# Polysketch attention with a multiplicative FFN: w3 loaded in row blocks, warm-up, key features and instruction order changed

## The chip, the cores and the metric

The kernel runs on one core of one Trainium2 chip. The metric is device time in microseconds (us), the median of three runs. A profiled execution gives the span from the first to the last instruction and the rows that are read below.

## The reference

Inputs q, k, v are (4, 4, 1088, 32), S1 and S2 are (8, 32), w1 and w2 are (128, 1024), w3 is (1024, 1024), w_out is (1024, 128). q, k, v are float32; S1, S2 and the weights come as float64, which the kernel reads as pairs of 32-bit words.

```python
def phi(x):                       # 64 features from 32 numbers
    a = np.einsum('rd,bhsd->bhsr', S1, x)
    b = np.einsum('rd,bhsd->bhsr', S2, x)
    return np.einsum('bhsi,bhsj->bhsij', a, b).reshape(*x.shape[:-1], r * r)
q_p, k_p = phi(q), phi(k)
kv = np.einsum('bhsf,bhsd->bhfd', k_p, v)
z = np.sum(k_p, axis=2)
num = np.einsum('bhsf,bhfd->bhsd', q_p, kv)
den = np.einsum('bhsf,bhf->bhs', q_p, z)[..., None] + 1e-06
attn_out = num / den
x = attn_out.transpose(0, 2, 1, 3).reshape(4352, 128)
out = ((x @ w1) * (x @ w2)) @ w3 @ w_out
```

## The kernel before

The whole program is a set of named steps, each of which issues one or a few instructions on one engine (or one or a few transfers). `ORDER`, a long string of step names, says in which order they are issued; every engine works its own instructions strictly in that order, and so does each engine's transfer queue. A step that must wait holds all later steps of its engine.

**Weights.** There are eleven weight tiles of 128 x 1024 words of 64 bits: w0 and w1 hold halves of w1 and w2 together, w2 is w_out, w3 to w10 are the eight row blocks of w3. Step `wN.load` (in `conv`) brings a tile into `raw`, of which there are three buffers. ACT turns it into float32 in three steps, `wN.c` (L325, upper word scaled), `wN.s` (L329, sign bits) and `wN.m` (L333, lower word); DVE finishes with `wN.j` (L344) and `wN.a` (L349). The `raw` buffer is free after `wN.c` and `wN.m`. The tiles of w3 are loaded in four transfers that each fill 32 partitions.

**Folding.** w3 and w_out are multiplied first: for each block ko, `fK.t` (DVE, L377) transposes the w3 tile in 32 x 32 blocks, `fK.m` (PE, L383) makes eight products with `wo`, and `fK.o` (ACT) puts the result into `w3o`.

**FFN.** The 4352 rows are worked in eight groups g0 to g7 of 512 columns and a rest gr of 256. For each group and each of eight column blocks c: `gG.Ca` and `gG.Cb` (PE, L1099 and L1109) make the products with w1 and w2, `gG.Cc` (ACT, L1104) copies the first, `gG.Cm` (DVE, L1115) multiplies the two into an `ab` tile (17 buffers), and `gG.Co` (PE, L1121) adds its product with `w3o[c]` to the group's output. `gG.oT` transposes the output, and `gG.st` stores it in four transfers; the output tile has one buffer.

**Attention.** For batch b the `kB.` steps make the key side. `kB.max`, `kB.lead` and `kB.rest` split k in a coarse and a fine part, `kB.gram0` to `gram2` sum its outer products (PE, L492), and a chain of small steps (`G..`, `T..`, `N..`) makes scaled projections from them. `kB.kT`, `kB.ab` and `kB.kp` make the features, `kB.kv` multiplies them with v, and `kB.kz` is what a query needs of a batch. `krM.` steps do the last 64 rows of two batches. `qG.` steps make the query side of group G, ending with `qG.x` (PE) and `qG.xT` (ACT), whose output `xT` the FFN products of group G read. For batch 0 the features `k0.kp0` and `k0.kp1` are made by GpSimd (POOL), one instruction each (L515).

**Zero products.** Steps `warm0` to `warm8` give PE products of zeros with zeros (L176), as many as `WARM` says, at places set in `ORDER`. They lie ahead of the first FFN product.

**Transfers** are all issued by SP, but for the two loads of k for batch 0, which ACT issues.

Of the kernel before, what the change touches and what calls it, by code (L numbers as in the profile page):

```python
# [25 lines left out]
WARM = [15, 5, 3, 1, 6, 15, 4, 2, 5]  # L26
# [7 lines left out]
c.zeros v0.zero c.ident c.mask k0.zero k0.load0 k0.loadr k0.load1 s.load c.act q0.load s.zero v0.loadr w0.load  # L34
k0.max0 w1.load k0.max1 k0.nat1 kr0.load warm0 k0.tr1 k0.g0 k0.g1 k0.lead0 k0.kT1 k0.lead1 kh1.load k0.nat0
k0.rest0 s.words k0.rest1 warm1 k0.gram0 s.pair q0.tr s.split k0.gram1 q1.tr s.lead w0.c v0.load q0.max k0.tr0
k0.Gm s.T k0.Gt k0.kT0 w0.j k1.zero s.P k1.load q0.l2 s.blk k0.Ga s.blkh warm2 k0.ab1 k0.Gb q0.l1 s.Pp k1.loadr
q0.A0 k0.ab0 w2.load q0.rm k0.T0 k0.T1 k0.abc0 kr0.tr k0.abc1 k0.Ta k0.kp0 warm3 q0.C0 w1.c k1.kT1 q1.max w1.m
k0.Tb q0.sma q0.restT kr0.kT k0.Ts w0.m k0.kp1 warm4 k0.kv0 k1.max k0.N0 k0.N1 w0.s q0.sta w3.load k0.Na q0.sha
w1.s k0.Nh k0.Nb q0.sla kr1.load warm5 q0.A1 k0.Nl k0.Nf kr0.ab q0.sca k0.kv3 q0.smy kr0.abc q0.al k0.kv1 kr0.kp  # L40
q0.sty q0.C1 q0.phi w4.load q1.l2 k0.kv2 k0.kvr v1.zero q1.l1 q0.shy warm6 q0.pt0 k0.kvm q0.C1t q0.sly k0.kzt
q0.pt1 q0.pc0 q0.scy v1.load q0.p01 q1.A0 k0.kz q0.pc1 q0.p2 warm7 q0.x q1.rm q0.p12 w1.j w3.c q0.dn q0.de w2.c
q1.sm q1.C0 q0.rc q1.st q0.xs w0.a q0.xt q0.xT q1.sh w2.m k1.g w1.a warm8 g0.1a g0.1b w2.j g0.1c w5.load w2.s
k1.lead g0.0a g0.1m kr1.tr g0.6a kr1.kT g0.0c k1.rest w3.s g0.0b w2.a kr1.ab g0.6b g0.6c w3.m g0.5a g0.0m g0.6m
g0.7a g0.5c w6.load q1.sl kr1.abc k1.kT0 g0.5b w3.j g0.7b g0.5m q1.load w4.c k1.gram0 w3.a g0.7c k1.ab w4.m
q1.sca q1.scy f0.t k1.gram1 w5.c w7.load k1.gram2 q1.al q1.p01 g0.2a q1.p2 w4.s k2.zero g0.7m q1.p12 kh2.load
g0.4a w4.j g0.2c q1.dn f0.m g0.4c w4.a w6.c k2.load q1.de k1.Gm f1.t v1.loadr w5.m g0.2b g0.4b q1.rc g0.2m f0.o
w5.s w10.load f1.m k1.Gt q1.bs q2.tr w6.m q1.phi g0.0o k1.abt f1.o w6.s w8.load q1.pt1 k1.Ga q2.max q1.pt0 w5.j
g0.3a q1.pc0 g0.4m q1.pc1 k2.loadr q1.x k1.kp1 g0.1o q1.xT w5.a q2.l2 g1.1a g0.3c k1.Gb g0.3b f2.t g1.1c q2.l1
k1.T0 k1.T1 g1.5a g0.3m f2.m k1.Ta g1.5c k1.kp0 w7.c w7.m w6.j g1.1b k1.Tb g1.6a w6.a f2.o w7.s w9.load k1.kv0  # L50
g1.1m k1.kv2 k1.kv3 k1.kv1 w8.c w7.j k1.kvr g0.2o f3.t w8.s g1.5b w7.a f3.m g1.6c k1.kvm k1.Ts g1.5m w8.j g1.6b
f3.o f4.t k1.N0 w9.c k1.N1 g1.4a g1.6m g1.4b k1.Na g1.4c k2.max w9.s f4.m g1.4m w8.m k1.Nb g1.0a k2.g w9.j f4.o
g1.0b k1.Nf q2.rm g1.0c w10.c k2.lead g0.3o k1.Nl k1.Nh g1.3a g1.0m k2.rest g1.2a g1.3c w9.m g0.4o q3.tr w8.a
k2.gram0 k2.gram1 k2.kT1 q2.C0 f5.t k2.kT0 k2.gram2 q3.max q2.A0 k2.ab k3.zero k3.loadr v2.zero w9.a kr1.kp
q3.l2 v2.load f5.m g1.2c q2.At q3.l1 q2.Ct q2.sm q3.rm g1.7a f5.o w10.s q2.st f6.t g1.3b w10.m g0.5o q2.sh w10.j
f6.m q2.sl g1.3m q2.sca q2.scy q2.al q3.A0 q2.p01 f6.o q3.C0 g1.7c w10.a g1.2b q2.p2 f7.t g1.7b q2.p12 q2.dn
f7.m k2.Gm q2.de q1.restT q2.rc q2.load q2.bs q3.At v2.loadr q3.Ct g0.6o kh3.load q2.phi f7.o g0.7o k2.abt
q2.pt0 k3.load g0.oT q2.pt1 g1.2m k1.kzt g1.0o g0.st k1.kz q2.pc0 q3.sm g1.7m q2.pc1 g1.2o k2.Gt q3.st g1.5o
q3.sh q3.sl q2.x k2.kp0 g1.3o q2.xT q3.sca k3.max g2.7a g2.1a k3.g k2.Ga q3.p01 k2.kp1 g2.7b g2.1c g2.7c g1.1o
q5.tr g1.6o q5.max q3.al k3.lead g1.4o q4.tr g1.7o k2.Gb g2.5a g2.7m q4.max g2.1b q3.scy k3.rest g2.5b k2.kv0  # L60
q3.p2 k3.gram0 g2.1m q3.p12 g2.5c k3.gram1 k3.kT0 g2.5m k2.kv3 k2.kv1 k2.kv2 g1.oT k2.kvr k3.gram2 v3.zero
v3.load k2.kvm q3.dn k2.T0 k2.T1 g2.2a k3.Gm k2.Ta g2.3a k2.Tb v3.loadr g2.2c k2.Ts q3.de q4.l2 g1.st q3.rc
k2.N0 q3.bs k2.N1 q3.phi g2.2b q4.l1 g2.3c g2.0a g2.2m k2.Na g2.3b g2.0c k2.Nb q3.pt1 k2.Nh k3.kT1 g2.0b g2.3m
q3.pt0 q4.rm g2.6a k2.Nf g2.0m g2.4b g2.6c k3.Gt k2.Nl q3.pc0 g2.4a q3.pc1 q3.x q4.A0 q3.xT q4.C0 g2.4c k3.ab
g2.0o k3.abt g2.4m g3.3a g2.6b g2.2o g2.6m k3.Ga g3.3b q4.At g3.3c q4.sm g2.5o q4.st q4.Ct g3.2b g3.3m q4.sh
g3.2a k3.kp0 k2.kzt g2.1o g3.2c q5.l2 g3.2m g3.4a k3.kp1 g2.4o g3.4c k2.kz q4.sl q5.l1 g3.4b q4.sca k3.Gb g3.6a
q4.p01 g3.4m q5.A0 q4.al k3.T0 k3.T1 g3.1a k3.Ta q5.At g2.6o q4.scy g3.1c q5.sm g3.6c q5.rm g3.1b q2.restT
q3.load g2.3o g3.1m k3.Tb g3.0b q4.p2 q4.p12 g3.6b q4.dn q4.de k3.Ts q5.st g3.0a q5.sh q3.restT g2.7o g3.0c
g3.0m q5.C0 q4.rc g3.6m q5.sl k3.kv0 k3.kv1 g2.oT k3.kv3 k3.kv2 q4.bs k3.kvr g2.st q5.Ct g3.5a q5.sca q5.p01
g3.7b g3.5c q6.tr g3.0o q4.phi g3.5b k3.kvm q7.tr g3.3o q5.al qr.max g3.2o q5.scy qr.l2 g3.5m q5.p2 q4.pt0  # L70
q5.p12 g3.6o q5.dn q4.pc0 qr.l1 g3.7a q4.pt1 g3.7c g3.1o q4.pc1 g3.7m q4.x q5.de q5.rc q5.bs g3.4o q4.xT k3.N0
k3.N1 g4.3b k3.Na qr.rm g4.3a k3.Nh k3.Nf k3.Nb q5.phi g4.0a g4.3c g3.5o g4.3m g4.0c q5.pt0 g4.5a g4.5b g4.5c
q5.pc0 q5.pt1 g4.5m g3.7o q5.pc1 g4.0b g4.4a g4.0m g3.oT g4.4b g4.4c g3.st g4.2a g4.4m k3.Nl g4.7a q6.max g4.0o
qr.C0 qr.A0 q5.x qr.Ct qr.At q7.max g4.5o q5.xT qr.sm g4.2c g4.2b g4.7c q6.l2 g4.7b g4.2m q6.l1 qr.st g5.0a
g4.7m qr.sh g4.6a g5.0c qr.sl q6.rm k3.kzt g4.6b qr.sca k3.kz g4.6c qr.al qr.p01 g5.0b g4.6m q6.A0 g5.0m q6.C0
q6.At qr.scy qr.p2 q7.l2 g4.1a qr.p12 qr.dn qr.de qr.rc g4.2o g4.1c q7.l1 g4.6o q7.rm g4.3o q6.sm qr.bs g4.1b
g5.2a g4.1m qr.phi g5.2b g5.2c q6.st qr.pt0 q6.sh g5.7a qr.pc0 q6.sl q6.Ct g4.4o g5.2m qr.pt1 q6.sca g4.1o
qr.pc1 q6.al g5.7c g5.7b q7.A0 q7.C0 q7.At q6.p01 g5.7m qr.x q6.scy q6.p2 q6.p12 g5.5a q6.dn q6.de q6.rc g4.7o
g5.5c q6.bs g5.6a g4.oT g5.6b g4.st g5.6c qr.xT g5.0o g5.6m q7.sm g5.5b q7.st g5.4a g5.5m q7.sh g5.4b g5.4c
q6.phi g5.5o q7.Ct g5.1a g5.4m q6.pt0 g5.3b q6.pc0 q6.pt1 g5.3a q6.pc1 g5.1c q6.x g5.3c g5.3m g5.1b q6.xT g5.6o  # L80
g5.1m q7.sl g5.4o q7.sca g5.1o g5.3o g6.1a g5.2o g6.1c g6.1b g6.4a g6.1m q7.scy g6.6a q7.al g6.4c q7.p01 g6.4b
g6.6c g5.7o g6.4m q7.p2 g6.6b g5.oT q7.p12 g6.0a g5.st g6.6m q7.dn g6.0b g6.0c g6.5a g6.0m g6.3a g6.5c g6.3b
g6.3c g6.5b g6.3m q7.de gr.2b g6.5m g6.0o q7.rc q7.bs g6.2a q7.phi gr.2a g6.2c g6.4o gr.2c gr.2m g6.6o g6.2b
gr.0a g6.2m q7.pt1 gr.0b gr.0c q7.pt0 gr.0m g6.7a q7.pc0 g6.7b g6.7c q7.pc1 q7.x g6.7m g6.5o q7.xT g7.1a g7.1b
g7.1c g7.0a g7.1m g6.2o g7.3a g6.3o g7.3c g7.0c g7.0b g6.1o g7.0m g6.7o g7.3b g6.oT g7.4a g6.st g7.3m g7.4b
g7.4c g7.2b g7.4m g7.2a g7.6a g7.2c g7.2m g7.0o g7.6c g7.2o g7.5a g7.1o g7.5c g7.6b g7.7a g7.6m g7.5b g7.7c
gr.5a g7.5m g7.7b gr.6a g7.7m g7.5o gr.6c gr.5c g7.3o gr.6b gr.5b g7.6o gr.5m gr.6m gr.4b gr.4a g7.4o gr.4c
gr.4m gr.1b gr.1a g7.7o gr.1c gr.1m gr.3a g7.oT gr.3b gr.3c gr.7a g7.st gr.3m gr.0o gr.7c gr.6o gr.2o gr.5o
gr.7b gr.3o gr.7m gr.1o gr.4o gr.7o gr.oc gr.ot gr.oT gr.st
# [7 lines left out]
def make_steps(ctx, tc, q, k, v, S1, S2, moe_w1, moe_w2, moe_w3, moe_w_out, out):  # L97
    nc = tc.nc
    dve, act, pe, pool, sp = nc.vector, nc.scalar, nc.tensor, nc.gpsimd, nc.sync
    B, H, S, D = q.shape  # L100
    r = S1.shape[0]
# [190 lines left out]
    def conv(n):  # L292
# [3 lines left out]
        def _():  # L296
# [4 lines left out]
            elif n == 2:  # L301
                for t in range(4):
                    sp.dma_start(raw[n][t * 32:(t + 1) * 32],
                                 bass.AP(tensor=moe_w_out.tensor, offset=moe_w_out.offset + t * 256 * DM,
                                         ap=[[DM, 32], [32 * DM, NC], [1, DM]]))
            elif n - 3 in BY_PE:
                sp.dma_start(raw[n], moe_w3[(n - 3) * 128:(n - 2) * 128])
            else:
                for t in range(4):
                    sp.dma_start(raw[n][t * 32:(t + 1) * 32],  # L310
                                 bass.AP(tensor=moe_w3.tensor, offset=moe_w3.offset + (n - 3) * 128 * DF + t * 256,
                                         ap=[[DF, 32], [32 * DF, 4], [1, 256]]))
# [898 lines left out]
```

## Time and profile before

| | us |
|---|---|
| median of 3 runs (279.46 to 284.89) | 280.36 |
| the profiled execution | 279.55 |
| its span | 277.70 |
| PE busy | 261.6 (94%) |
| DVE busy | 186.0 (67%) |
| ACT busy | 113.0 (41%) |
| POOL busy | 11.6 (4%) |

Busy time counts an instruction from its start to its end; products on PE overlap, so that a busy PE is not PE at its peak. In the page of the profile the span is cut into 40 equal slices, 6.9 us each; a digit is the busy share of a slice in tenths. DMA is the mean busy share of the 16 DMA engines. 22.5 MB are moved in all, 19.9 MB of them read from memory, nearly all in the first 75 us. Rows of a timeline give start and duration in us, engine, line, operation, output and inputs, shape and count, and in brackets how long the engine was idle before and what ended it; "issue" there is time in which it waited for nothing that the profile shows.

### The profile page before, as it was taken

The numbers are of one execution on the slowest core, as the hardware profiler recorded it, in microseconds if no ns is written. First come the engines' busy times: TensorE is split into PE (matmuls) and PEld (weight loads), VectorE is DVE, ScalarE is ACT, GpSimd is POOL, SyncE is SP. The second block draws the span as 40 slices with busy tenths as digits, with TensorE's granted clock in tenths as the row PEclk, the third lists the DMA queues.
The fourth block names the chain that finished last, engine by engine and source line by source line (L and its number), as shares of the span: only waits on it lengthen the run. The fifth ranks groups of instructions, "written<-read, shape, count | busy, mean of one in ns | idle before, by whom it ended". The sixth has DMA issues, their size and how long they took to land.

```text
span 277.7 us, 5298 instructions
## 1 busy us (share of the span) xinstructions
PE 261.6 (94%) x2134; PEld 147.7 (53%) x2134; DVE 186.0 (67%) x420; ACT 113.0 (41%) x180; POOL 11.6 (4%) x41
## 2 busy tenths in 40 slices
PE   7997899699998999979999999999999999999992
PEld 5886646446657663634444544444544445344571
DVE  4779989699889999965597944576772264132330
ACT  3576599676592522034132134154223222322121
POOL 2451000000001000000000000000000000000000
PEclk9999999999999999999999999999999999999998
DMA  7999989999500273050002200200020020011011
GB/s 202 341 257 210 206 192 251 211 218 200 123 1 19 66 211 65 2 120 0 2 0 81 40 0 0 40 0 1 2 38 0 0 41 0 0 19 19 0 21 38
DMA packets 32168, 22.50 MB, mean 81 GB/s; under 512 B 21392, under 2 KB 26640, under 8 KB 32144
## 3 DMA queue, kind: packets, MB, share of 16 engines
q1 hardware_dynamic: 31600, 21.64, 34.8%
q10 hardware_dynamic: 544, 0.52, 0.6%
q8 instruction: 17, 0.28, 0.5%
q14 instruction: 7, 0.06, 0.1%
HBM read 19.93 MB, written 2.23 MB: 80 GB/s over the span
## 4 chain that ended last, share of the span: by engine, by line
PE 68%; DMA 22%; SPq 3%; ACT 3%; issue 2%; DVE 0%; ACTq 0%
PE ps_o L1121 19%; PE a_ps L1099 18%; PE b_ps L1109 18%; DMA raw<-in_moe_w_dram 15%; DMA k<-in_k_dram 6%; PE ps_c L810 3%; PE ps_w3o L383 3%; PE ps_x L1065 3%; PE ps_ph L1020 2%; PE ps_g L492 1%; SPq L1077 1%; ACT sg L333 1%; ACT cv_c L325 1%; PE ps_kv L590 1%; DMA out_dram<-oT 1%
## 5 line engine op out<-in xcount | busy, mean ns | idle before, releaser
L1115 DVE TENSOR_TENSOR ab<-ffa,b_ps 128x512 f32<-128x512 f32 (+1 forms) x72 | 46.9, 652 | 59.3 <-PE b_ps L1109 45.5
L1104 ACT COPY ffa<-a_ps 128x512 f32<-128x512 f32 (+1 forms) x72 | 39.9, 565 | 97.0 <-PE a_ps L1099 85.4
L1099 PE MATMUL a_ps<-xT,w 128*128 128x512 f32 (+1 forms) x144 | 69.1, 575 | 1.6 <-ACT xT L1057 1.2
L1109 PE MATMUL b_ps<-xT,w 128*128 128x512 f32 (+1 forms) x144 | 68.8, 572 | 0.0
L1121 PE MATMUL ps_o<-ab,w3o 128*128 128x512 f32 (+1 forms) x144 | 67.4, 574 | 0.0
L1109 PEld LDWEIGHTS b_ps<-xT,w 128*128 128x128 f32 x144 | 26.4, 190 | 28.4 <-issue 24.9
L1099 PEld LDWEIGHTS a_ps<-xT,w 128*128 128x128 f32 x144 | 25.8, 190 | 27.5 <-issue 20.2
L1121 PEld LDWEIGHTS ps_o<-ab,w3o 128*128 128x128 f32 x144 | 26.1, 190 | 26.2 <-issue 23.1
L383 PEld LDWEIGHTS ps_w3o<-wo,w3T 128*128 128x128 f32 x128 | 15.5, 192 | 6.6 <-issue 5.4
L383 PE MATMUL ps_w3o<-wo,w3T 128*128 128x128 f32 x128 | 16.1, 277 | 2.4 <-issue 2.4
L325 ACT ACTIVATE cv_c<-raw 128x1024 f32<-128x1024 f32 x11 | 12.8, 1174 | 7.2 <-DMA raw<-in_moe_w_dram 7.2
L333 ACT ACTIVATE sg<-raw 128x1024 uint16<-128x1024 uint32 x11 | 15.2, 1380 | 0.0
L329 ACT CAST sg<-cv_c 128x1024 f16<-128x1024 f32 x11 | 15.0, 1378 | 0.0
L1026 ACT COPY pT<-ps_ph 128x512 f32<-128x512 f32 (+1 forms) x18 | 9.9, 566 | 7.4 <-PE ps_ph L1020 7.2
L492 PE MATMUL ps_g<-kk 128*32 128x64 f32 x288 | 10.8, 232 | 1.8 <-issue 1.8
L1020 PEld LDWEIGHTS ps_ph<-ident,ph 128*128 128x128 f32 x68 | 8.2, 141 | 6.8 <-issue 4.6
L492 PE MATMUL ps_g<-k,kk 128*32 128x32 f32 x288 | 10.3, 200 | 1.1 <-issue 1.1
L176 PE MATMUL idle_ps<-zeros 128*128 128x256 bf16 x56 | 9.8, 326 | 1.1 <-DVE zeros L151 1.1
L492 PEld LDWEIGHTS ps_g<-kk 128*32 128x32 f32 x288 | 9.0, 114 | 3.2 <-issue 1.9
L492 PEld LDWEIGHTS ps_g<-k,kk 128*32 128x32 f32 x288 | 9.6, 116 | 1.9 <-issue 1.9
L1020 PE MATMUL ps_ph<-ident,ph 128*128 128x128 f32 x68 | 10.1, 274 | 0.0
L377 DVE STREAM_TRANSPOSE w3T<-w3c 128x1024 f32<-128x1024 f32 x8 | 9.9, 1235 | 0.0
(199 smaller groups left out, 290.9 us busy)
## 6 DMA issues: line engine op xcount, KB each, us to landing
raw<-in_moe_w_dram SPq DMA_DIRECT2D x32, 256.0 KB, 7.9
qh<-in_q_dram SPq DMA_DIRECT2D x4, 544.0 KB, 4.1
raw<-in_moe_w_dram SPq DMA_DIRECT2D x4, 512.0 KB, 6.1
out_dram<-oT SPq DMA_DIRECT2D x32, 64.0 KB, 2.0
kh<-in_k_dram SPq DMA_DIRECT2D x12, 128.0 KB, 6.8
k<-in_k_dram SPq DMA_DIRECT2D x3, 512.0 KB, 7.3
v<-in_v_dram SPq DMA_DIRECT2D x12, 128.0 KB, 2.8
raw<-in_moe_w_out_dram SPq DMA_DIRECT2D x4, 256.0 KB, 8.0
```

The source lines that it names most:

```text
L325: act.mul(shape(x["c"], 1, True), words(1).bitcast(F32), 2.0 ** -112)
L329: act.copy(bview(sign_bits[n % 2].bitcast(F16)[:, 1:], [[2, 1024]]), x["c"])
L333: act.mul(shape(sign_bits[n % 2].bitcast(U16), 2, True), words(0).bitcast(U32), 2.0 ** -29)
L377: dve.transpose(w3T[ko].rearrange("p s (i r) -> p s i r", r=32), bview(w3c[ko], [[32, NC], [256, 4], [1, 32]]))
L383: pe.matmul(t["o"], w3T[ko][:, c], wo[:, c], start=c == 0, stop=c == NC - 1)
L492: pe.matmul(o[h * D:(h + 1) * D], lhs, rhs, start=start, stop=stop, skip_group_check=True)
L1020: pe.transpose(t[:, j * 128:(j + 1) * 128], ph_cols(j, p), ident)
L1099: pe.matmul(x["a"][:, :w], w_of(0, c), xT[g][:, c0:c0 + w], start=True, stop=True)
L1104: act.copy(x["s"][:, :w], x["a"][:, :w])
L1109: pe.matmul(x["b"][:, :w], w_of(1, c), xT[g][:, c0:c0 + w], start=True, stop=True)
L1115: dve.tensor_mul(ab_sb[g, c][:, c0:c0 + w], x["s"][:, :w], x["b"][:, :w])
L1121: pe.matmul(o_ps[g][:, :n], w3o[:, c], ab_sb.pop((g, c))[:, :n], start=c == 0, stop=c == NC - 1)
```

## The change

Four things change. The w3 tiles are still loaded in four transfers each, of the same size, but one transfer now takes 32 whole rows of w3 and fills 256 columns of all 128 partitions. The zero products are 19, 5, 2, 3, 18, 6 and 5 in seven places, where they were 15, 5, 3, 1, 6, 15, 4, 2 and 5 in nine. The features of batch 0 are made by GpSimd in halves (`k0.kp0a`, `k0.kp0b`, `k0.kp1a`, `k0.kp1b`). And `ORDER` is another one; to allow for it, the transposed keys `kT` are kept by batch. No other step is different.

```diff
-WARM = [15, 5, 3, 1, 6, 15, 4, 2, 5]
+WARM = [19, 5, 2, 3, 18, 6, 5]
...
-                for t in range(4):
-                    sp.dma_start(raw[n][t * 32:(t + 1) * 32],
-                                 bass.AP(tensor=moe_w3.tensor, offset=moe_w3.offset + (n - 3) * 128 * DF + t * 256,
-                                         ap=[[DF, 32], [32 * DF, 4], [1, 256]]))
+                for i in range(4):
+                    sp.dma_start(raw[n][:, i * 256:(i + 1) * 256],
+                                 bass.AP(tensor=moe_w3.tensor, offset=moe_w3.offset + ((n - 3) * 128 + i * 32) * DF,
+                                         ap=[[256, 4], [DF, 32], [1, 256]]))
...
-                @step(f"k{b}.kp{half}")
-                def _(half=half):
-                    f["kp", half] = sb("kp", [128, 4 * H, r, r], bufs=2)
-                    x = f["abs", half]
-                    k_phi(f["kp", half], x[:, 0], x[:, 1], pool)
+                for part in "ab":
+                    @step(f"k{b}.kp{half}{part}")
+                    def _(half=half, part=part):
+                        if part == "a":
+                            f["kp", half] = sb("kp", [128, 4 * H, r, r], bufs=2)
+                        x, g = f["abs", half], slice(0, 2 * H) if part == "a" else slice(2 * H, 4 * H)
+                        k_phi(f["kp", half][:, g], x[:, 0, g], x[:, 1, g], pool)
```

In a pattern such as `[[DF, 32], [32 * DF, 4], [1, 256]]` each pair is a step and a count, the outermost first.

The order of SP's first loads was k0 rest, S, q0, v0 rest, w0, w1, kr0, kh1, v0, k1, k1 rest, w2, w3, kr1, w4, v1, w5, w6, q1, w7, kh2, k2, v1 rest, w10, w8, k2 rest, w9. It is now k0 rest, S, q0, kh1, kr0, w0, k1, k1 rest, v0, w1, w3, v0 rest, w2, k2, w5, kr1, w4, w7, v1, k2 rest, q1, w6, kh2, w8, w9, v1 rest, k3, w10. (khB is k once more in another layout, for `kB.kT`.)

The opening of the new order up to the first FFN products, and its end:

```
c.zeros c.ident s.zero k0.zero k0.load1 k0.loadr k0.load0 c.mask s.load c.act q0.load kh1.load k0.max1 kr0.load
k0.max0 k0.nat0 s.words warm0 k0.tr0 k0.g0 k0.lead0 w0.load k0.g1 k0.rest0 k0.lead1 warm1 k0.gram0 s.pair
...
k0.kT1 k0.kp0a k0.Gb k1.max k0.kp0b kr0.tr k0.T0 k0.T1 kr0.kT w0.c k0.Ta v0.zero v0.load w1.load w3.load
v0.loadr q0.sma w0.m k1.g w0.j k0.Tb q0.sta w0.s warm4 k0.N0 k0.Ts w2.load k1.lead k0.ab1 q0.sha k1.rest w1.c
k0.N1 k0.kv0 kr0.ab k0.kv1 k0.Na kr0.abc w1.m k1.gram0 kr0.kp q0.sla k0.Nb k1.gram1 q0.sca w1.s k0.Nf k0.Nh w0.a
q0.A1 k0.abc1 k0.Nl q0.C1 q0.al w3.c q0.smy k0.kp1a k1.kT1 q0.sty q1.l2 q0.phi k0.kp1b warm5 k0.kv2 k1.gram2
q1.l1 q0.shy k0.kv3 q0.C1t k2.zero k2.load k0.kvr q0.sly q0.pt0 k0.kvm w5.load v1.zero q0.scy q1.A0 q0.p01
k0.kzt q0.pc0 q0.pt1 w1.j k1.ab k0.kz q0.pc1 q0.p2 w1.a w2.c kr1.load q0.x q0.p12 w3.s q1.rm q0.dn q1.C0 q0.de
k1.abt w3.m q0.rc k1.Gm q0.xs w4.load q1.sm q0.xt w3.j q0.xT w2.j w2.s warm6 g0.4a k1.Gt q1.st w3.a g0.4b g0.4c
...
g7.2o gr.6a gr.6b gr.6c g7.1o gr.6m g7.7o gr.5a g7.oT gr.5b gr.5c gr.4a g7.st gr.5m gr.4b gr.4c gr.0o gr.4m
gr.5o gr.6o gr.1o gr.7a gr.7b gr.7c gr.2o gr.7m gr.4o gr.3o gr.7o gr.oc gr.ot gr.oT gr.st
```

In the order before, `k1.gram0`, `k1.ab`, `k1.gram1`, `k1.gram2`, `k1.lead`, `k1.rest`, `w0.a` and `w1.a` came after `q0.xs`, and `k1.load` came after `w1.load` in SP's queue.

## The prediction

> **What bounds the kernel now.** I read the page's slices first, then the chain of work that ended last, then stretches and single rows. The slices show two halves of different kind: until slice 11 (some 75 us) the DMA engines are full at about 210 GB/s, and from slice 12 on they have little to do.
>
> ```profile
> span 277.7 us, 5298 instructions
> PE 261.6 (94%) x2134; PEld 147.7 (53%) x2134; DVE 186.0 (67%) x420; ACT 113.0 (41%) x180; POOL 11.6 (4%) x41
> DMA  7999989999500273050002200200020020011011
> GB/s 202 341 257 210 206 192 251 211 218 200 123 1 19 66 211 65 2 120 0 2 0 81 40 0 0 40 0 1 2 38 0 0 41 0 0 19 19 0 21 38
> ```
>
> The chain in order of time says the same: up to 70.9 us it is nearly all transfers, the weights above all, and from 74 us on it is products without a pause.
>
> ```profile
> 20.91 10.08 DMA raw<-in_moe_w_dram
> ...
> 36.37 6.14 DMA raw<-in_moe_w_dram
> ...
> 44.06 7.75 DMA raw<-in_moe_w_dram
> 51.88 8.92 DMA k<-in_k_dram
> 61.17 9.70 DMA raw<-in_moe_w_dram
> 70.94 1.15 ACT cv_c L325
> ```
>
> This chain alone would say that faster weight transfers bring 20 us. The timeline of PE forbids that. The first wide product (a_ps, step g0.1a) starts at 33.8 us, and from there PE has work nearly always, because eight plus eight a/b pairs need no w3. The largest hole left in the opening is 2.4 us, in the middle of f0.m, and it is no wait for data ("issue").
>
> ```profile
> 33.82 1.13 PE L1099 MATMUL a_ps<-xT,w 128*128 128x512 f32 x2 [1.21 <-ACT xT L1057]
> 51.02 1.05 PE L383 MATMUL ps_w3o<-wo,w3T 128*128 128x128 f32 x7 [2.37 <-issue]
> 97.60 1.95 PE L383 MATMUL ps_w3o<-wo,w3T 128*128 128x128 f32 x16
> ```
>
> The third of these rows is f7.m, the last fold of w3. It starts at 97.60 us, though the last w3 tile had landed by 75 us: some 20 us of slack. From f7.m to the end of the span lie 277.67 - 97.60 = 180.1 us of products. So less transfer time can give only what PE still loses; much more transfer time eats the slack first, and then moves f7.m and the end with it, one for one.
>
> **The change part by part.** Costs are set against the profiled execution, 279.55 us (span 277.70, 1.85 around it); the median is 0.8 us above it.
>
> *w3 transfers (L309 to L312).* A tile is 128 x 1024 x 8 bytes = 1.049 MB in four transfers, before and after, the same bytes to the same places. Before, one filled 32 partitions; its source pattern begins with 32 rows. After, one fills 256 columns of all 128 partitions; its source pattern is [[256, 4], [DF, 32], [1, 256]], beginning with a count of 4. Two stretches give the price:
>
> ```profile
> 8.00:12.00 4.00, 4.00 (x138) 3.88 (x133) 2.61 (x9) 1.53 (x3) 3.20 (x8) 1.00 1.01 386
> 60.00:66.00 6.00, 6.00 (x30) 3.57 (x29) 5.17 (x13) 4.77 (x8) 0.00 (x0) 1.00 1.06 213
> ```
>
> The last columns are DMA share and GB/s. From 8 to 12 us w0 and w1 land over 128 partitions: 386 GB/s, 24.1 per engine. From 60 to 66 us w3 lands over 32 partitions with all engines just as busy: 213 GB/s, 13.3 per engine. If all 16 engines carry the new transfers, a tile takes 1.049/0.386 = 2.7 us instead of 4.9. If a transfer is dealt to engines by the first count of its patterns, only 4 carry it: 10.9 us at 24.1 GB/s each, 19.7 us at 13.3 each. All data loads of before but the two 2 KB loads of S begin with 32 or more on both sides, so no row shows a first count of 4. [...]
>
> [...]
>
> *What 10.9 us a tile makes of the opening.* I add up the loads in SP's new order, each at its stretch's rate; engines work their lists in order, so the busiest four carry every load. k0 and q0 are in by 6.5 us (204 GB/s over the first 7 us in the stretch from 0 to 7). Then kh1 0.52 MB at 213: 2.5; kr0 0.3; w0 2.7; k1 and v0 1.05 MB at 297 (stretch 14 to 18, such loads): 3.5; w1 2.7. w1 is in at 18.2. Up to w10 there remain, besides w3: w2 4.9 (32 partitions), k2 and k3 3.5, v1 and kh2 4.9, q1 1.4, small rests 0.5: 15.2. Eight tiles are 87.2. Last tile in: 18.2 + 15.2 + 87.2 = 120.6 us. The three raw buffers add nothing: w4's comes free at w3.m near 38 us, while the list is full to 46. From there w10 needs c 1.15, s and m 1.37 each, a 1.22, t 1.24 (rows L325, L329, L333, L349, L377; j lies beside): 6.4. f7.m at 127.0 instead of 97.6.
>
> PE's demand: with the medians of before as step costs, f7.m comes 54 us after the first wide product in the new order (57 in the old). From 34 us that would be 88, so PE waits 39 us in all, spread over f3, f5, f6 and f7. What is queued behind f.m on PE waits too, and ACT and DVE behind their w.c and f.t.
>
> *Zero products (WARM, 56 to 58).* The first block grows from 15 to 19, at 3.38/15 = 0.23 us each 0.9 us more; it covers 4.44 to 5.28, where PE idled 0.75 us. k0.tr0 comes 0.1 us later at most. The products before 9.7 us run at half pace (0.21 us against 0.11 later); if the closed gap ends that earlier, the first gram gains up to 1.2 us. The key features, DVE and w0 come after it in line: I count 0, bounds +0.2 and -1.2.
>
> *Key features in parts.* kp0 and kp1 take POOL 3.87 us together; kpr of a quarter of the size takes 0.63, so a half costs about 1.07 and cutting adds 0.2 to each. While kp0 ran to 18.0, DVE's T_p (L137) took 1.73 us, its likes 0.18. A half can hold DVE for one half at most: gain up to 1.5 us in k0's T chain, used in the next sum.
>
> *The order.* DVE before q0.xs gets w0.a, w1.a, k1.lead, k1.rest, k1.kT0, k1.abt, k1.Gm: 5.8 us by their starts in before; q0.restT, q1.sm, q1.st leave it: -0.9. Waits that stood there and need not: 1.33 for ps_g, 0.55 for ps_T, 0.94 for k1's load (now ahead of w1) and 1.55 for T_p. Sum +0.5: first wide product at 34.3; bounds 33.8 and 39. For that, k1.gram and k1.ab (42.97 to 45.66, 2.7 us of PE) now lie before it under warm-up and waits. The stall in f0.m follows 88 small products; these are gone from there, but may stall elsewhere: -1.2, bounds 0 and -2.4. At the end g7.oT gets 14 half-width products behind it instead of 12, so its store is through 0.9 us earlier against PE's last product: -0.9.
>
> **Sum.** 127.0 + 180.1 - 0.9 = 306.2 span, 308.0 with the 1.85 around it, 309 on the scale of the median. The -2.7 and -1.2 do not count here: they are spent in waiting. Ends: 8 x 19.7 us give 380; at the other end w2, v1 and kh2 may run at the full pace once the idle engines have done their share, -4.9, so 304. If PE's long waits bring back the half pace that its products show before 9.7 us, a few us come on top; the range holds them.
>
> **The rivals.** *All 16 engines carry it (not slower).* For it: nothing in the trace shows a transfer that does not fill them. Then f7.m no longer waits and PE's own sum decides: 279.55 + 0.5 - 2.7 - 1.2 - 0.9 = 275.3, 276 on the median's scale, 271 to 281 by the bounds. It decides as soon as a tile costs under about 6 us: (34 + 54 - 6.4 - 18.2 - 15.2)/8. The 15 us by which the loads shrink bring nothing by themselves: PE was fed.
> *The new order starts the wide products late.* If DVE keeps its waits before q0.xs, 5 us more work stand ahead of them: 275.3 + 4.5, 280; no visible change. Against it: the waits named are for things that now come earlier.
> [...]
>
> **How the numbers follow.** Four engines 0.74, of which 0.12 near the slow end above 365; sixteen engines 0.20; late start 0.06. The likeliest gives 309 (its own range 304 to 365). Up to 365 and down to 274 leaves out about 0.12 above and 0.07 below. Faster by over 2% (under 274.8; 2% is about what a measurement of this kernel can tell) is the lower part of the sixteen-engine case: 0.08. Within 2%: its rest and most of the late start: 0.16. Slower: 0.76.
>
> **What would show it.** Right: from 20 to 115 us the DMA share falls to a third or less at some 100 GB/s while w3 tiles are still coming; f7.m near 127 us; waits on PE and ACT for raw in the tens of us; 180 us from f7.m to the end. The rest stands alone: T_p near 0.2 to 1.2 us, k1.gram before the first wide product, that one near 34 to 38 us (ACT's w3.c and w2.c now stand ahead of q0.xT). Wrong: 350 GB/s or more in the w3 slices and f7.m near 90 us; then it is the sixteen-engine case, and if f7.m is late in spite of that, the order.

## The result, and the profile after

The changed kernel takes 316.8 us (median of four, 315.39 to 319.14) against 280.62 us (279.46 to 284.89): a ratio of 1.131, 95% interval 1.120 to 1.142. It is slower by some 36 us; the forecast was 309. One run of before took 284.89 us, 1.5% above the median of the same kernel, and the ratios are of runs without such ones. The profiled execution is the longest of the four, 319.14 us with a span of 317.4 us.

The page first: the rows that were read before, and PEclk, the granted clock of TensorE in tenths of full speed, which was at nines in every slice but the last before.

```profile
span 317.4 us, 5304 instructions
PE 277.8 (88%) x2136; PEld 158.1 (50%) x2136; DVE 185.7 (59%) x420; ACT 112.5 (35%) x180; POOL 13.3 (4%) x43
PEclk9998558859778978999999999999999999999999
DMA  7965632253422331250205100200200200201011
GB/s 185 257 215 153 148 105 99 102 168 108 127 100 101 129 123 59 69 147 0 39 2 139 35 1 0 33 2 1 33 2 0 33 1 2 33 0 21 12 26 26
```

Where the DMA row had mostly nines up to slice 10 (some 70 us), it now has twos to fives from slice 6 to slice 15 (some 40 to 119 us), and the rate comes back to 100 GB/s again and again. Two stretches in which w3 tiles make up nearly all of the traffic, with DMA share and GB/s in the last columns and the granted clock ahead of them:

```profile
52.00:64.00 12.00, 6.47 (x17) 2.51 (x16) 5.64 (x11) 4.26 (x7) 0.00 (x0) 0.86 0.26 102
100.00:104.00 4.00, 4.00 (x22) 2.65 (x21) 2.63 (x4) 2.78 (x5) 0.00 (x0) 1.00 0.26 102
```

A quarter of the engines' time, 102 GB/s: four engines at 25.5 GB/s each. (That it is four full engines, and not sixteen at a quarter of their pace, shows in the completions that the trace records as a transfer lands: each new w3 transfer has four of them, each old one 16.) A tile of 1.049 MB takes 10.3 us. The chain that ended last, in order of time:

```profile
17.34 18.88 DMA raw<-in_moe_w_dram
...
62.33 13.60 DMA v<-in_v_dram
76.52 15.07 DMA raw<-in_moe_w_dram
...
100.75 13.44 DMA v<-in_v_dram
...
118.11 3.79 PE ps_w3o L383 x16
...
139.00 1.78 PE ps_w3o L383 x16
```

The v loads between the raw ones are the point: 32 KB of v1's last rows (issued at 100.75) need 13.44 us, because they stand in the queue behind w3 tiles: twelve of their 16 completions come at 106.43 to 106.91 us, the other four at 111.16 to 114.18, each 0.18 to 0.25 us behind one of the four completions of the w3 transfer ahead (110.91 to 114.00). PE's timeline at five places (start, duration, and in brackets the idle time before and what ended it):

```profile
36.51 0.44 PE L599 MATMUL ps_kv<-kpr,v 128*32 128x64 f32 x8 [6.87 <-DMA v<-in_v_dram]
...
50.87 1.13 PE L1101 MATMUL a_ps<-xT,w 128*128 128x512 f32 x2
...
64.70 2.08 PE L1101 MATMUL a_ps<-xT,w 128*128 128x512 f32 x2 [6.23 <-ACT ffa L1106]
...
80.05 1.09 PE L1022 MATMUL ps_ph<-ident,ph 128*128 128x128 f32 x8 [4.29 <-DVE ph L1011]
...
138.84 1.95 PE L383 MATMUL ps_w3o<-wo,w3T 128*128 128x128 f32 x16
```

The first wide product starts at 50.87 us instead of 33.82, f7.m at 138.84 instead of 97.60. From there to the end lie 317.4 - 138.84 = 178.6 us, 1.5 less than before. So the whole loss is made before f7.m. PE's longest wait, the first row, is for the last rows of v0, again 32 KB that stand behind a w3 tile; for those of v1 it waits 2.86 us ahead of 114.32. In its other long waits ACT or DVE released PE, and these had waited for transfers. ACT's timeline shows it:

```profile
36.32 1.13 ACT L325 ACTIVATE cv_c<-raw 128x1024 f32<-128x1024 f32 x1 [9.34 <-DMA k<-in_k_dram]
...
62.88 1.34 ACT L333 ACTIVATE sg<-raw 128x1024 uint16<-128x1024 uint32 x1 [6.58 <-DMA raw<-in_moe_w_dram]
...
114.07 1.13 ACT L325 ACTIVATE cv_c<-raw 128x1024 f32<-128x1024 f32 x1 [9.49 <-DMA raw<-in_moe_w_dram]
...
126.03 1.16 ACT L325 ACTIVATE cv_c<-raw 128x1024 f32<-128x1024 f32 x1
...
134.22 1.37 ACT L333 ACTIVATE sg<-raw 128x1024 uint16<-128x1024 uint32 x1
```

Each of the first three is a conversion step for a tile not yet in, and ACT works in order: q0's copies, an a-copy for g0.2a and the a-copy of g1.2 stand behind them. (The first row names k; w3.c reads the w3 tile alone, and a wait is named after the transfer that came last by the profile.) The last two rows are w10.c and w10.m: 8 us lie between the first and the last ACT step of the last tile.

### The profile page after: what moved, and what is told of

Its sections match the earlier page's. It is cut to its first block, busy times and chain, and to the rows that moved or that the text cites. A ratio compares the mean times of both kernels' runs of the same rounds, so it can differ in the third digit from the quotient of the medians.

```text
span 317.4 us, 5304 instructions
## 1 busy us (share of the span) xinstructions
PE 277.8 (88%) x2136; PEld 158.1 (50%) x2136; DVE 185.7 (59%) x420; ACT 112.5 (35%) x180; POOL 13.3 (4%) x43
## 2 busy tenths in 40 slices
DMA packets 31784, 22.50 MB, mean 71 GB/s; under 512 B 21008, under 2 KB 26256, under 8 KB 31760
## 4 chain that ended last, share of the span: by engine, by line
PE 65%; DMA 20%; SPq 6%; ACT 3%; issue 2%; DVE 1%; POOL 1%; ACTq 0%; DVEq 0%
PE ps_o L1123 18%; PE b_ps L1111 15%; PE a_ps L1101 15%; DMA raw<-in_moe_w_dram 11%; DMA v<-in_v_dram 9%; SPq L310 5%; PE ps_w3o L383 4%; PE ps_c L812 2%; PE ps_x L1067 2%; PE ps_ph L1022 2%; PE ps_ab L567 1%; PE ps_xt L1041 1%; DMA k<-in_k_dram 1%; ACT sg L333 1%; ACT sg L329 1%
## 5 line engine op out<-in xcount | busy, mean ns | idle before, releaser
L1101 PE MATMUL a_ps<-xT,w 128*128 128x512 f32 (+1 forms) x144 | 70.2, 587 | 12.3 <-ACT ffa L1106 12.3
L1111 PE MATMUL b_ps<-xT,w 128*128 128x512 f32 (+1 forms) x144 | 70.3, 582 | 0.0
L383 PEld LDWEIGHTS ps_w3o<-wo,w3T 128*128 128x128 f32 x128 | 19.9, 239 | 7.7 <-ACT ffa L1106 3.6
L383 PE MATMUL ps_w3o<-wo,w3T 128*128 128x128 f32 x128 | 20.1, 324 | 3.5 <-ACT ffa L1106 3.5
L1022 PE MATMUL ps_ph<-ident,ph 128*128 128x128 f32 x68 | 10.9, 292 | 4.3 <-DVE ph L1011 4.3
L140 DVE TENSOR_REDUCE k_g<-k 128x1 f32<-128x1152 f32 (+1 forms) x5 | 5.5, 1110 | 11.9 <-DMA k<-in_k_dram 11.9
L492 PE MATMUL ps_g<-kk 128*32 128x64 f32 x288 | 10.1, 238 | 0.5 <-DVE kk L484 0.5
L349 DVE CUSTOM_DVE_ANT_0 w3c<-w3c,sg 128x2048 uint16<-128x2048 uint16 x8 | 9.6, 1221 | 1.2 <-ACT sg L329 1.0
L599 PE MATMUL ps_kv<-kpr,v 128*32 128x64 f32 x32 | 1.4, 245 | 9.7 <-DMA v<-in_v_dram 9.7
```

The source lines that it names most:

```text
L383: pe.matmul(t["o"], w3T[ko][:, c], wo[:, c], start=c == 0, stop=c == NC - 1)
L492: pe.matmul(o[h * D:(h + 1) * D], lhs, rhs, start=start, stop=stop, skip_group_check=True)
L1022: pe.transpose(t[:, j * 128:(j + 1) * 128], ph_cols(j, p), ident)
L1101: pe.matmul(x["a"][:, :w], w_of(0, c), xT[g][:, c0:c0 + w], start=True, stop=True)
L1111: pe.matmul(x["b"][:, :w], w_of(1, c), xT[g][:, c0:c0 + w], start=True, stop=True)
```

## The experiments

The theory of the prediction, A: a w3 transfer runs on as many engines as its source pattern's first count, and this alone is the loss. The rivals: B, it is not the count but the old bytes or the old column blocks; C, the form over all 128 partitions or its issue on SP is slow (SP's median for one w3 issue went from 424 to 1070 ns); D, the new order costs.

**One form, three first counts.** Three kernels differ in one pair of numbers; c is 4, 8 or 16.

```diff
-  offset=moe_w3.offset + ((n - 3) * 128 + i * 32) * DF,   ap=[[256, 4], [DF, 32], [1, 256]]
+  offset=moe_w3.offset + (n - 3) * 128 * DF + i * 256,    ap=[[DF, c], [c * DF, 128 // c], [1, 256]]
```

> The changed kernel, with other rows in the w3 transfers: each still fills 256 columns of all 128 partitions with 2 KB pieces, but the 128 pieces are now one block of columns of 128 rows, read as [[DF, 4], [4*DF, 32], [1, 256]]: first count 4, rows 0, 4, 8 and so on first (what lands is not the arrangement that the folds need, so the output is left out of account). Theory A, the first count of the source deals a transfer to that many engines: as in the changed kernel, about 102 GB/s with a DMA share of 0.26 while w3 comes, 10.3 us a tile, 315 to 319 us. Rival B, the old bytes are what is slow (four column blocks of the same 32 rows in one transfer): 276, share near 1. Rival C, the form over all 128 partitions or its issue on SP is slow, whatever the count: 317 here and in its two sisters with counts of 8 and 16.

> The same pieces and places as the kernel with a first count of 4, read as [[DF, 8], [8*DF, 16], [1, 256]] (not the folds' arrangement). Theory A: eight engines, 204 GB/s and a share of 0.51, 5.1 us a tile, which is about the price of before; the last fold no longer waits long, and PE's own sum decides: 276 to 282 us. Rival C (form or issue): 317.

> The same pieces and places again, read as [[DF, 16], [16*DF, 8], [1, 256]] (not the folds' arrangement). Theory A: all 16 engines, some 386 GB/s and a share near 1, 2.7 us a tile, and yet no more than 3 us less than with a first count of 8, because PE is fed either way: 274 to 280 us. Rival C: 317. If 16 is faster than 8 by over 5 us, the slack that I gave a tile (up to 6 us) was wrong.

(The three kernels compute other numbers than the reference, since rows of w3 land in other partitions; each step does the same work.) Measured: 4: 317.4 us, ratio 1.125 (1.116 to 1.133). 8: 288.5 us, ratio 1.012 (1.000 to 1.023). 16: 278.3 us, ratio 0.985 (0.977 to 0.994). The stretches in which w3 tiles come, for 4, 8 and 16 in turn (DMA share and GB/s last):

```profile
84.00:96.00 12.00, 6.92 (x24) 4.51 (x22) 6.12 (x8) 4.90 (x6) 0.00 (x0) 0.72 0.26 99
```

```profile
70.00:76.00 6.00, 5.22 (x15) 1.92 (x15) 5.68 (x9) 4.13 (x5) 0.00 (x0) 1.00 0.52 195
```

```profile
51.00:61.00 10.00, 9.83 (x42) 5.15 (x41) 8.31 (x15) 8.43 (x14) 0.00 (x0) 1.00 1.09 261
```

Share 0.26, 0.52, 1.09, and the trace has 4, 8 and 16 completions for a transfer (in all 31784, 31912 and 32168 packets, so that each of the 32 w3 transfers has 4 and 12 more with c = 8 and 16 than with c = 4): the same bytes into the same tile in transfers of the same size, and only the first count, with the order of rows that it makes, differs. B and C are out: C expected 317 three times, and a kernel with other column blocks but a first count of 4 is as slow as the changed one. Theory A holds at 4, at 8 and at 16. No run tries a count that does not divide 128. The 386 GB/s expected with 16 are not seen: its stretch has 261, with q1 and the keys for the transposed copy of k2 among the w3 tiles.

One expectation fell. I had given a tile 6 us before it would cost anything; 8 engines need about 5.4 (1.049 MB at 195 GB/s), and the ratios are 2.6% apart, some 7 us. The kernel with 8 shows where, on DVE and then on PE:

```profile
64.38 1.35 DVE L140 TENSOR_REDUCE k_g<-k 128x1 f32<-128x1152 f32 x1 [7.46 <-DMA raw<-in_moe_w_dram]
65.65 1.22 DVE L1011 TENSOR_TENSOR ph<-s_al,s_bs 128x1024 f32<-128x1024 f32 x1
```

```profile
66.92 1.33 PE L1022 MATMUL ps_ph<-ident,ph 128*128 128x128 f32 x5 [6.06 <-DVE ph L1011]
```

DVE stood in k2.max with q1.phi behind it, and PE's q1.pt0 waited for q1.phi. k2.max reads k2, whose last rows SP had issued at 53.38 us, behind a w3 tile and v1. With 16 engines the same wait of PE is 0.17 us. The tile time was not too long for the folds; it was too long for a small load queued behind it. The four times of the kernel with 8 spread from 284.3 to 290.4 us, and this profile is of the run of 289.9: that the wait of 6 us makes up the 7 us between the ratios fits, but it was not tested by itself.

**The new transfers in the old order.** The kernel before, with only L309 to L312 as in the change.

> The kernel before, with nothing changed but the w3 transfers. Theory A: the four-engine transfers are the whole loss, in any order: eight tiles at 10.3 us put f7.m between 125 and 140 us instead of 97.6, and 180 us follow it: 307 to 322 us. Rival D, the new order (conversions ahead of the first wide product, loads queued behind w3) is what costs: at most 290 here.

Measured: 325.4 us, ratio 1.152 (1.143 to 1.162); f7.m at 141.80. D is out: the old order loses more. There k2.max comes at 116.0 us, and PE loses 18 us in one piece ahead of g1.6b, at 94 to 112 us. It is 3 us above the range that I gave.

**The old transfers in the new order.** The changed kernel with the old lines:

```diff
-  for i in range(4): sp.dma_start(raw[n][:, i * 256:(i + 1) * 256], ... ap=[[256, 4], [DF, 32], [1, 256]])
+  for t in range(4): sp.dma_start(raw[n][t * 32:(t + 1) * 32], ... ap=[[DF, 32], [32 * DF, 4], [1, 256]])
```

> The changed kernel with the w3 transfers of before (32 partitions, first count 32); order, zero products and key features stay new. Theory A, the four engines are the whole loss: the loss goes. My blind sum for a tile at 4.9 us or less was 276. The run with a first count of 8 (5.1 us a tile) was near 287 and the one with 16 at 278, so I now expect 280 to 286, with DVE's wait for k2's keys behind w3 tiles as the difference to 278. Rival D, the new order itself costs: over 290.

Measured: 278.3 us, ratio 0.988 (0.982 to 0.994). All of the loss is gone and some 3 us more: by its interval this version is a little faster than the kernel before too, by 1.2%, less than the 2% that the prediction takes as what a measurement of this kernel can tell. It also shows a part of my working by itself:

```profile
26.32 1.16 ACT L325 ACTIVATE cv_c<-raw 128x1024 f32<-128x1024 f32 x1 [5.59 <-DMA raw<-in_moe_w_dram]
...
29.87 0.37 ACT L546 COPY kab<-ps_ab 128x256 f32<-128x256 f32 x1
...
30.56 1.12 ACT L325 ACTIVATE cv_c<-raw 128x1024 f32<-128x1024 f32 x1 [0.32 <-DMA raw<-in_moe_w_dram]
```

```profile
41.74 1.12 PE L1101 MATMUL a_ps<-xT,w 128*128 128x512 f32 x2
...
98.65 1.61 PE L383 MATMUL ps_w3o<-wo,w3T 128*128 128x128 f32 x13
```

Without any four-engine transfer the first wide product still comes at 41.7 us, where I had said 34.3 and at most 39. The new order puts w1.c and its sisters ahead of ACT's k0.abc1 (kab, 29.87); before, k0.abc1 stood ahead of w1.c. GpSimd's kp1 halves, and PE's kv2 and q0.pt0, come after k0.abc1. And yet f7.m is only 1 us later than before (98.65 against 97.60): 56.9 us after the first wide product instead of 63.8, which fits with small products that now lie ahead of it.

**A second queue.** Of a tile's four old transfers, GpSimd issues those to partitions 64 to 127; once in the new order, once in the kernel before.

```diff
-  for t in range(4):           sp.dma_start(raw[n][t * 32:(t + 1) * 32], ...
+  for t in (0, 2, 1, 3):       (sp, pool)[t // 2].dma_start(raw[n][t * 32:(t + 1) * 32], ...
```

> The same, but of the four transfers of a w3 tile those of partitions 0 to 63 are issued by SP and those of 64 to 127 by GpSimd, in turn, so that an engine has pieces for both halves of the partitions at hand. [...] If an engine works its queues one after the other, or the pieces themselves are slow, the rate stays near 213 and the time that of the kernel with SP alone, or worse by GpSimd's own issue times ahead of its key features.

> The kernel before with the w3 transfers on two queues in the same way, nothing else changed. My prediction says that faster w3 transfers bring nothing to the kernel before, since PE was fed (20 us of slack for the last fold): 0.99 to 1.01 of before, even if the rate rises to some 386 GB/s. The rival reading, by the chain of waits, which is nearly all transfers up to 71 us: faster by up to 10 us.

Measured: in the new order 278.1 us, ratio 0.991 (0.987 to 0.995), beside 0.988 with SP alone; in the kernel before 281.4 us, ratio 1.000 (0.996 to 1.004). The rate does not rise. SP alone, then both queues, both in the new order:

```profile
51.00:61.00 10.00, 10.00 (x43) 5.30 (x41) 8.36 (x15) 8.62 (x14) 0.00 (x0) 1.00 1.09 237
```

```profile
51.00:61.00 10.00, 10.00 (x32) 4.22 (x30) 9.34 (x11) 6.62 (x10) 1.09 (x2) 1.00 1.04 238
```

So this is a failed way to faster old transfers, and it cannot test whether faster transfers would have helped the kernel before. The kernel with a first count of 16 comes nearest to that: 261 instead of 237 GB/s, and the same time as the old transfers within the intervals.

**Loads moved ahead.** For the 12 us by which f7.m is later than forecast I first blamed two waits for loads.

```diff
-  g0.5c w7.load ... v1.load ... k2.loadr ... w6.load kh2.load ... v1.loadr
+  g0.5c kh2.load w7.load ... v1.load ... v1.loadr k2.loadr ... w6.load
```

> The changed kernel, four-engine transfers and all, with two loads moved ahead in SP's order: k2's keys for the transposed copy ahead of w7, and v1's last rows right behind v1. Theory A1, the miss on f7.m (138.8 instead of 127 us) comes from work that waits in order behind loads queued after w3 tiles (DVE's k2.max at 4.5 us of PE, v1's rows at 6.5 us), while the last tile itself comes at 124.5: f7.m at 131 to 135 and 310 to 314 us, not less, as the last tile and 6.4 us of conversion now set it. Rival A2, the last tile and ACT's order set f7.m in any case: no change from the changed kernel, 315 to 319.

Measured: 316.9 us, ratio 1.128 (1.121 to 1.135), f7.m at 136.30: no change that can be measured. (The profile of the changed kernel is of its longest run; the kernel with c = 4, which has the changed kernel's order, has f7.m at 136.10.) A1 fell, for two reasons that its waits show (us in total, times, longest):

```profile
DVE k_g L138 <- DMA k<-in_k_dram: 12.2, 3, 8.4
...
ACT cv_c L323 <- DMA raw<-in_moe_w_dram: 11.5, 2, 9.9
```

DVE's reduction reads k2 itself, not the transposed copy whose load I moved, so it waits as before (11.9 us in three times in the changed kernel). And the wait for v1's rows is gone, but another stood right behind it: PE now idles 6.78 us ahead of f4.m, released by an a-copy that ACT had held behind w9.c.

```profile
111.52 1.12 ACT L323 ACTIVATE cv_c<-raw 128x1024 f32<-128x1024 f32 x1 [9.88 <-DMA raw<-in_moe_w_dram]
...
114.90 0.60 ACT L1104 COPY ffa<-a_ps 128x512 f32<-128x512 f32 x1
```

**ACT's wait moved behind.** The same kernel, with w9's c, s, m and j behind f3 and f4:

```diff
-  ... g1.4c w9.c g1.2a ... w9.s ... w9.m ... w9.j ... f3.o f4.o ... q2.rm w10.c
+  ... g1.4c g1.2a ... f3.o f4.o ... q2.rm w9.c w9.s w9.m w9.j w10.c
```

> The kernel with the two loads moved ahead (four-engine transfers), in which moreover ACT's and DVE's first steps on the tile of w9 (c, s, m, j) stand behind f3 and f4 instead of ahead of them. With the two loads alone PE lost nothing at v1's rows any more and 6.9 us at f4.m instead, while ACT, which works in order, stood for 9.9 us in w9.c until that tile was in, with the a-copies that PE's a/b pairs need behind it. Theory A3, it is this wait in order, plus the 21 us of products between f4.m and f7.m, that puts f7.m at 136 to 139: without it f4.m starts before 112 us and f7.m at 131 to 134 us, where the last tile (in at 124 us) and its conversion hold it: 308 to 313 us. Rival A2, the bytes on four engines set f7.m however the work is ordered: 315 to 318.

Measured: 315.5 us, ratio 1.121 (1.116 to 1.126); f4.m at 108.39, f7.m at 133.87.

```profile
123.83 1.12 ACT L324 ACTIVATE cv_c<-raw 128x1024 f32<-128x1024 f32 x1 [5.72 <-DVE s_hl L956]
...
128.35 1.37 ACT L332 ACTIVATE sg<-raw 128x1024 uint16<-128x1024 uint32 x1
```

In the trace it goes as A3 says: f4.m before 112, f7.m 2.4 us earlier than with the loads alone and 2.2 earlier than in the kernel with c = 4, and w10.c starts as the last tile comes in (its last completion is recorded at 123.73 us; the row names the DVE step that ended last). In time it is not separated: the median is 1.3 us below that of the changed kernel, the intervals of the two ratios overlap, and it lies above the 308 to 313 that I gave, inside the 315 to 318 of A2. The bytes on four engines leave that little to the order.

**The opening of the better version.** In the new order with the old transfers, v0's last rows ahead of w1, and k0.abc1, kp1a and kp1b ahead of w1.c; with SP alone and with both queues.

```diff
-  v0.load w1.load w3.load v0.loadr ... k0.ab1 q0.sha k1.rest w1.c ... kr0.abc w1.m ... q0.A1 k0.abc1 ... k0.kp1a ... k0.kp1b
+  v0.load v0.loadr w1.load w3.load ... k0.ab1 k0.abc1 k0.kp1a k0.kp1b q0.sha k1.rest ... kr0.abc w1.c w1.m ... q0.A1
```

> The changed kernel with the old w3 transfers (278, and a first wide product at 41.7 us), with an order in which v0's last rows are loaded ahead of w1, and ACT's copy k0.abc1 and GpSimd's kp1a and kp1b stand ahead of w1.c, which waits 5.6 us for w1 and held them; w1.c stands behind kr0's copy. Theory E, ACT's wait in order holds the opening: k0's products kv2 and kv3 start near 28 instead of 31.4 us, the first wide product at 37 to 39, and the time falls by 2 to 4 us, to 274 to 276. Rival F, the next tiles or DVE take the place of this wait, as f2 is fed just in time: no change, 277 to 279.

> The same order with the w3 transfers of partitions 64 to 127 issued by GpSimd. If rival F holds for the kernel above because the tiles come too late for an earlier start, this one, whose w3 tiles come faster, shows the gain: 274 to 276. If the gain is there in both, the queues add nothing and both have the same time within 1 us.

Measured: 277.7 us, ratio 0.988 (0.983 to 0.993), and 278.4 us, ratio 0.989 (0.984 to 0.994). No gain. kp1a did start earlier, at 26.1 instead of 30.3 us, but the first wide product came at 43.7 instead of 41.7. The granted clock (third column from the end) differs; first this kernel with SP alone, then its sister without the edit:

```profile
14.00:18.00 4.00, 4.00 (x20) 3.99 (x20) 2.93 (x8) 0.86 (x2) 1.65 (x2) 0.52 0.89 265
18.00:22.00 4.00, 4.00 (x22) 3.09 (x23) 1.91 (x10) 2.47 (x4) 0.65 (x2) 0.50 0.87 243
22.00:26.00 4.00, 4.00 (x33) 2.99 (x35) 2.47 (x6) 1.62 (x3) 0.00 (x0) 0.70 1.06 185
```

```profile
14.00:18.00 4.00, 4.00 (x38) 3.76 (x38) 2.80 (x8) 1.86 (x4) 2.30 (x3) 1.00 0.90 273
18.00:22.00 4.00, 3.38 (x41) 2.76 (x38) 3.90 (x14) 2.73 (x3) 0.00 (x0) 1.00 1.02 250
22.00:26.00 4.00, 2.64 (x114) 2.43 (x110) 3.17 (x13) 0.00 (x0) 0.00 (x0) 0.59 1.08 215
```

The stretch at half pace came at 14 us instead of 22, on work that stands ahead of the key products that the edit wanted early: 18 zero products take 4.02 us instead of 2.14, and k0.ab1 starts at 24.45 us instead of 20.28. The sister with two queues has it at 14 us too (0.54 and 0.50). This can have used up the gain; no run has the edit without it. Neither E nor F had this in it; what moves that stretch is left open.

**The zero products alone.** The better version with a first block of 15 products instead of 19.

> The changed kernel with the old w3 transfers and a first block of 15 zero products instead of 19, so that PE again has a gap of some 0.9 us ahead of k0.tr0. In the two runs with 19 products the granted clock was full from 6.0 us, with 15 (the kernel before) from 9.7. If the gap decides that, k0.gram0 takes 2.8 instead of 1.8 us here; my blind count for it in the whole was nothing (between -0.2 and +1.2 us for this kernel against its sister with 19). Expected: full pace later, and 277 to 280 us, no difference to the sister that can be measured. If the zero products were the source of the 1.2% that the new order brings with the old transfers, this one is back at 281.

Measured: 279.1 us, ratio 0.990 (0.985 to 0.995). PE's first products, with 15 and with 19:

```profile
1.06 3.38 PE L176 MATMUL idle_ps<-zeros 128*128 128x256 bf16 x15 [1.06 <-DVE zeros L151]
5.23 1.09 PE L529 MATMUL ps_kt<-ident,nat 128*128 128x128 f32 x4 [0.78 <-ACT nat L523]
6.11 1.27 PE L176 MATMUL idle_ps<-zeros 128*128 128x256 bf16 x5
7.31 0.44 PE L492 MATMUL ps_g<-kk 128*32 128x64 f32 x4
```

```profile
1.06 4.23 PE L176 MATMUL idle_ps<-zeros 128*128 128x256 bf16 x19 [1.06 <-DVE zeros L151]
5.36 0.77 PE L529 MATMUL ps_kt<-ident,nat 128*128 128x128 f32 x4
5.96 0.71 PE L176 MATMUL idle_ps<-zeros 128*128 128x256 bf16 x5
7.06 0.31 PE L492 MATMUL ps_g<-kk 128*32 128x64 f32 x4 [0.39 <-DVE kk L484]
```

With 15 products and the gap of 0.78 us behind them the full pace comes later: the next five zero products take 1.27 us instead of 0.71, and the Gram products keep the slow pace until 9.4 us. Whether the gap does it, or the four products fewer, this run does not separate. In the whole it makes no difference that can be measured.

## Why the prediction was right, and where its steps failed

*The deal by the first count.* Right, shown by the series of 4, 8 and 16. The pace of an engine, taken at 24.1 GB/s from the stretch with w0 and w1, is 25.5; a tile takes 10.3 us, not 10.9. That a first count of 4 means four engines was an assumption that no row of before shows; the series shows it of the source's count, and why this decides, with 128 partitions on the other side, no run shows. The slow end (13.3 GB/s, 380 us) is excluded by the same rows.

*Last tile in at 120.6.* The other loads were mis-sized. The last completion of w10 is recorded at 125.93 us in the changed kernel, 5.3 us late, and at 123.0 to 123.7 in the three other four-engine kernels of (nearly) this order (c = 4 and the two with moved steps). In the profiled run of the changed kernel one of the four engines completes this tile 2.0 us after the other three; no run shows why. The tiles themselves were cheaper by 0.6 each, eight of them 82.4 us: so the other loads took 43.5 us, not 18.2 + 15.2 = 33.4. Part of it lies ahead of the first w3 tile, as w1 is in at 22.9 instead of 18.2. That the sum came within 5 us is in part luck, as the two errors have opposite signs.

*"From there w10 needs c, s, m, a, t: 6.4."* This step failed, and it is the larger part of the miss of 11.8 us on f7.m: w10.c starts at 126.03, 0.1 us after the tile is in, and from there to f7.m the changed kernel needs 138.84 - 126.03 = 12.8 us. I took the path to run through the last tile and a chain of durations. The path that the trace shows runs through the tile before: ACT stands in w9.c until 114.07, the a-copy behind it releases PE at 118.11 for f4.m, and from there PE works without a pause through 20.7 us of products to f7.m. w10's own steps wait on this: w10.m is behind f6.o, which waits for f6.m. The kernel with c = 4 shows the same, with 12.6 us from w10.c (at 123.46, as its tile comes in) to f7.m; here are its f4.m and f7.m:

```profile
115.54 3.71 PE L383 MATMUL ps_w3o<-wo,w3T 128*128 128x128 f32 x16 [3.45 <-ACT ffa L1106]
...
136.10 1.95 PE L383 MATMUL ps_w3o<-wo,w3T 128*128 128x128 f32 x16
```

In the kernel with w9 moved, where the path does run through the last tile, it is 10.0 us. So 5.3 us of landing and 6.4 us between the members of the chain give the 11.8 us between 127.0 and 138.8.

*"A few us on top" for the half pace.* It came back, as the prediction allowed: in the changed kernel the clock is at half in six stretches between 23 and 122 us, 48 us together. From 115 to 122 us it lies on the path just told (f4.m takes 3.8 us instead of 2.05 in the kernel with w9 moved). What it costs in all no run separates. That waits on PE bring it back was my estimate and is not shown.

*180 us after f7.m.* Held: 178.6. My 0.9 for the tail was 0.5 (PE idles 1.24 us ahead of gr.ot before, 0.70 after); a stall of 1.81 us in the middle of k3's Gram products (at 119.98 us before), which I had not priced, is gone.

*The first wide product at 34.3.* Failed by far: 50.87, and 41.74 even with the old transfers. The sum was made of DVE's steps; ACT's were left out, with w1.c, w3.c and w2.c ahead of copies that PE needs, and so was PE's wait for v0's last rows (6.87 us). In the changed kernel ACT stands 9.3 us in w3.c for its tile, and then the clock adds to it: from 42 to 50 us PE is busy all the time at a granted clock of 0.50, and q0.x and q1's products take 3.5 us each instead of 2.1 and 1.8.

```profile
42.00:50.00 8.00, 8.00 (x41) 7.75 (x38) 4.99 (x11) 2.48 (x3) 0.00 (x0) 0.50 0.30 107
```

The traces show no cost of it at the end: f7.m was tied to later tiles, and the four engines had pieces to move nearly all the time until the last tile was in (DMA share 0.26 or more in each 4 us from 20 to 120 us). The step costs were off as well: 57 us from the first wide product to f7.m in the old order are 63.8 in its own rows (97.60 - 33.82), and 54 in the new order are 56.9 with the old transfers. PE's waits did not lie at f3, f5, f6 and f7 as I wrote, but at v0's rows, at the first a/b pairs, at q1.pt0, at g1.1, at v1's rows and, of the folds, at f4: mostly steps behind other engines' waits in order.

*Zero products and key features.* As priced. The first block takes 0.86 us more and moves k0.tr0 by 0.1; the full pace comes earlier, and no worth of it can be measured in the whole. A half of kp takes 1.07 us, T_p 0.18, now with no half beside it. Beside a later half (27.06 to 29.16 us) one DVE step (L137, s_hiy) takes 0.91 us instead of 0.29, another (L1011) its usual 1.2.

*The rival with 16 engines.* Its 276 us (271 to 281) is what the runs give when the loss is taken away: 278.3 with 16 engines, 278.3 with the old transfers. Its point of decision, 6 us a tile, was wrong by at least 0.6, as 8 engines showed (some 5.4 us a tile). That some 1.2% remains as a gain of the new order with the old transfers is measured, though it is under 2%; of its 3 us the traces place some 1.5 behind f7.m, the rest is not located.

## What to carry to other kernels

Read the first count of a transfer's source pattern before its bytes: a loop of 4 put outermost turned sixteen engines into four here, and the DMA share (0.26, with 8 it was 0.52) says so at a glance. When transfers become late, ask of each in-order engine what stands behind the step that waits: the loss showed at small loads, at copies and at k2.max, and hardly at the folds that read the tiles. And do not add up a chain by its own durations alone; add what the order puts between its members.

## What the hardware showed that I had not expected

The granted clock falls to half within the program: 0.50 from 42 to 50 us in the changed kernel, 0.59 from 22 to 26 with the old transfers, 0.5 from 14 us after an edit that should have helped. In the first and the third of these the products take up to twice as long (q1's 3.5 us instead of 1.8, 18 zero products 4.02 instead of 2.14), and a later stretch falls on the path (f4.m 3.8 us instead of 2.05). The runs give no rule for it. In the 4 us ahead PE was busy 3.38 us in the second case and 3.12 in the third, and the kernel before kept its full clock from 9.7 us to 275.9 us with only 2.48 us busy from 22 to 26. Nor does the order of steps alone decide it: the kernel before with nothing but the second queue was at half from 16.1 to 29.7 us in its profiled run (mean clock 0.972, against 0.997 before). And two queues for the two halves of the partitions gave 238 GB/s where one gave 237.
